# Two thirds of the converted weights are packed inside their own tile and stored from there

## The chip, the cores and the metric

The kernel runs on one core of one Trainium2 chip. The metric is the device time of one execution in microseconds (us). A core has TensorE (PE, with its weight loads shown apart as PEld), VectorE (DVE), ScalarE (ACT), GpSimd (POOL) and SyncE (SP). POOL and SP issue most of the DMAs here; each engine takes its instructions in order and stops at one whose semaphore has not come.

## The reference

```python
scores = np.where(masks, scale * q @ k.T, -1e9)      # 4 x 8 heads, 576 tokens, 64 wide; local and strided masks
x = softmax(scores) @ v                              # 2304 tokens x 512
h = x @ w_in;  g = s * np.maximum(h, 0) ** 2 + b     # 512 -> 2048
x = g @ w_out                                        # 2048 -> 512
x = ((x @ w_a) * (x @ w_b)) @ w_out2                 # 512 -> 1536, twice; 1536 -> 512
```

All of it is wanted in float32. The six weight arrays come as float64, so each weight is two 32-bit words, a low and a high one, that the kernel turns into one float32 word.

## The kernel before

TensorE multiplies each float32 operand as a high and a low part, three products a piece. The first MLP walks over five blocks of tokens (n = 0 to 4) and, in each, over 16 slices f of 128 hidden columns. For one slice `h_mm` (matmuls `h`) fills a PSUM bank; ACT takes it out with the relu into the one tile `r` (L802) and squares it into `gt` (L809); DVE makes the low part (L812, L813); and `o_mm` (matmuls `acc`) uses `gt` two slices later. In blocks 1 to 3 the bank of `h` is a single one, so the next slice's `h` waits for the relu before it, and the relu waits until L813 has freed `r`. Between the slices stand the steps of the attention of later tokens: `pss` (scores), softmax pieces on DVE and ACT (L437 to L451), `ppt` (transposes on PE), `po` (values), and copies of `po` into the next block's `x` (ACT L122, DVE L124).

Also between the slices of blocks 1 to 3, `convert_w2` turns the second MLP's weights into float32: 36 pieces of 128 rows, i = 0 to 35, in the order w_a, w_b, w_out2, w_a and so on, so that i % 3 tells the kind (2 is w_out2). One conversion is:

- a load of 512 KB from DRAM into a tile `raw` [128, 512, 2] on POOL's queue (L130 for w_a and w_b, L135 for w_out2). There are two such tiles, used in turn, and the load of piece i + 2 is issued right behind the store of piece i;
- ACT scales the high words in place (L142), DVE shifts the low words (L145), joins bits of both into the low words (L148), and packs both into one float32 word (L158);
- a store of 256 KB to DRAM (`w2d`) on POOL's queue (L865).

In the kernel before, L158 writes to a tile of its own, `w2s`, of which there is one. A piece's ACT and DVE instructions may not start before the last instructions of the slice that stands ahead of them (`behind`); otherwise the order on each engine comes from the framework's scheduler, when the program is built. From block 4 on the stored weights are read back and combined for the second MLP, whose matmuls are `pp` and `o`.

Of the kernel before, what the change touches and what calls it, by code (L numbers as in the profile page):

```python
# [12 lines left out]
U32 = mybir.dt.uint32  # L13
# [7 lines left out]
P = 128  # L21
# [6 lines left out]
def sparse_attention_two_mlps(  # L28
# [16 lines left out]
    NT, DM = out.shape  # L45
# [23 lines left out]
    hp = ctx.enter_context(tc.tile_pool(name="hp", bufs=1))  # L69
# [23 lines left out]
    w2s = [dram.tile([P, 2, 2, DM], F32, name=f"w2s{i}") for i in range(NF2)]  # L93
# [10 lines left out]
    @contextmanager  # L104
    def after(instructions):
        with ExitStack() as st:
            for i in instructions:
                st.enter_context(tc.issue_after(i))
            yield
# [16 lines left out]
    def stage(w, f, cols, pool, eng=nc.sync):  # L126
        r = pool.tile([P, DM, 2], U32, tag="w" if pool in (wpa, wpb, wpc) else "raw", name="raw")
        words = w.bitcast(U32)
        if cols:
            load = eng.dma_start(  # L130
                out=r.rearrange("p (k c) t -> p k (c t)", k=KD),
                in_=words[:, f * 2 * P:(f + 1) * 2 * P].rearrange("(k p) c -> p k c", p=P),
            )
        else:
            load = eng.dma_start(  # L135
                out=r.rearrange("p c t -> p (c t)"), in_=words[f * P:(f + 1) * P, :]
            )
        return r, load.ins

    def to_float32(r, out=None, quarters=False):  # L140
        low, high = r[:, :, 0], r[:, :, 1]
        nc.scalar.activation(  # L142
            out=high.bitcast(F32), in_=high.bitcast(F32), func=AF.Copy, scale=HIGH_SCALE
        )
        nc.vector.tensor_scalar(  # L145
            out=low, in0=low, scalar1=29, scalar2=None, op0=ALU.logical_shift_right
        )
        nc.vector.scalar_tensor_tensor(  # L148
            out=low, in0=high, scalar=3, in1=low, op0=ALU.logical_shift_left, op1=ALU.bitwise_or
        )  # L150
        out = high if out is None else out
        pieces_ = [(out, high, low)]
        if quarters:
            to = out.rearrange("p (r a i c) -> p a r i c", r=2, a=2, c=STR)
            low, high = (t.rearrange("p (r i a c) -> p a r i c", r=2, a=2, c=STR) for t in (low, high))
            pieces_ = [(to[:, a], high[:, a], low[:, a]) for a in range(2)]
        for to, high, low in pieces_:
            nc.vector.scalar_tensor_tensor(  # L158
                out=to, in0=high, scalar=0x80000000, in1=low, op0=ALU.bitwise_and, op1=ALU.bitwise_or
            )  # L160
        return out.bitcast(F32)
# [689 lines left out]
    def convert_w2():  # L851
        words = {}

        def load(i):
            if i < 3 * NF2:
                f, kind = divmod(i, 3)
                words[i] = stage((w_a, w_b, w_o2)[kind], f, kind < 2, raw, nc.gpsimd)[0]

        load(0)
        load(1)  # L860
        yield
        for i in range(3 * NF2):
            with after(list(behind)):
                w = to_float32(words.pop(i), hp.tile([P, DM], U32, tag="w", name="w2s"), i % 3 == 2)
            nc.gpsimd.dma_start(out=w2d[i], in_=w)  # L865
            load(i + 2)
            yield
# [219 lines left out]
    words = []  # L1087
# [56 lines left out]
    for what in ORDER.split():  # L1144
        name, of = what[:-1], int(what[-1])
# [8 lines left out]
    for f, piece in enumerate(pieces):  # L1154
        wi[f] = by_rows(piece.w)
    later = [Stream(convert_w2(), 3 * NF2 + 1, sum(T1[1:-1]) * NF1 - 3 * T1[-2])]
    for n in range(1, NB):
        plan(n)
# [300 lines left out]
    for pair in range(NP2):  # L1459
        quads = []  # L1460
        later_x.clear()
        for g in range(NG2):
            i = pair * NG2 + g
            kind = g % 2
            w = loaded[i]
# [121 lines left out]
```

## Time and profile before

| | us |
|---|---|
| median of 3 runs | 881.11 (880.87 to 881.37) |
| the profiled execution, its own time | 882.01 |
| its span, from the first instruction to the last | 880.2 |
| PE busy in the span | 870.9 |
| POOL busy in the span | 158.1 |

The profiled execution is 0.9 us above the median and its span leaves out 1.8 us around the program. In the views of the profile a group of rows gives busy time, the mean of one instruction and the idle time of its engine ahead of it, with the instruction or DMA that ended that idle time behind an arrow.

### The profile page before, as it was taken

How to read it: one execution, taken by the hardware profiler on the slowest of the kernel's cores; microseconds unless marked ns; L12 is line 12 of the kernel's file. 1: busy time of each engine (PE TensorE's matmuls, PEld its weight loads, DVE VectorE, ACT ScalarE, POOL GpSimd, SP SyncE). 2: the span in 40 equal slices, each digit the busy share in tenths (PEclk: the TensorE clock that was granted, in tenths of full speed). 3: DMA queues.
4: the chain of work that ended last, by engine and by line, in shares of the span. 5: the costliest groups of instructions: out<-in, count | busy, mean ns of one | idle time of the engine just before them, and what ended most of it. 6: DMA issues, size and time to landing. Idle time of an engine off the chain costs nothing.

```text
span 880.2 us, 17207 instructions
## 1 busy us (share of the span) xinstructions
PE 870.9 (99%) x6296; PEld 805.4 (92%) x6296; DVE 679.1 (77%) x1363; ACT 406.4 (46%) x872; POOL 158.1 (18%) x308
## 2 busy tenths in 40 slices
PE   8999999999999999999999999999999999999998
PEld 6778888999888899998888999999999999999998
DVE  6898996686767676847876798798877797887794
ACT  6777774443433343337665333463223463222261
POOL 6000001111112211114544000005400005200020
PEclk9999999999999999999999999999999999999999
DMA  9975543866685758458999668688668788766487
GB/s 213 289 236 151 173 85 105 186 163 165 170 201 151 178 173 188 140 169 281 351 317 338 197 207 261 216 256 263 203 198 278 251 252 260 211 200 206 150 259 217
DMA packets 173156, 187.21 MB, mean 213 GB/s; under 512 B 108880, under 2 KB 125648, under 8 KB 173072
## 3 DMA queue, kind: packets, MB, share of 16 engines
q1 hardware_dynamic: 147776, 119.90, 47.7%
q0 software_dynamic: 20096, 64.90, 22.4%
q10 hardware_dynamic: 5200, 1.31, 0.8%
q8 instruction: 50, 0.82, 0.4%
q14 instruction: 34, 0.28, 0.1%
HBM read 143.59 MB, written 42.47 MB: 211 GB/s over the span
## 4 chain that ended last, share of the span: by engine, by line
PE 96%; ACT 2%; DVE 1%; issue 0%; POOL 0%; ACTq 0%; POOLq 0%
PE pp L99 30%; PE h L99 23%; PE acc L99 22%; PE o L99 15%; PE po L99 2%; PE pss L99 1%; PE ppt L102 1%; PE fpo L99 1%; ACT fpt L620 1%; PE lull L99 0%; ACT raw L142 0%; PE fps L102 0%; PE pst L102 0%; ACT fqkT L620 0%; PE fpp L102 0%; PE fss L99 0%
## 5 line engine op out<-in xcount | busy, mean ns | idle before, releaser
L99 PE MATMUL pp<-x2w,wf 128*128 128x384 f32 x1296 | 230.9, 334 | 0.0
L99 PEld LDWEIGHTS pp<-x2w,wf 128*128 128x128 f32 x1296 | 225.2, 188 | 0.1
L99 PE MATMUL h<-x,w 128*128 128x512 f32 (+1 forms) x960 | 215.8, 373 | 0.0
L99 PE MATMUL acc<-gt,w 128*128 128x512 f32 (+2 forms) x960 | 210.7, 368 | 1.0 <-ACT w L122 1.0
L99 PEld LDWEIGHTS acc<-gt,w 128*128 128x128 f32 x960 | 175.5, 188 | 24.0 <-ACT w L122 1.4
L99 PEld LDWEIGHTS h<-x,w 128*128 128x128 f32 x960 | 172.5, 188 | 24.5 <-DVE w L124 0.5
L99 PE MATMUL o<-gf,o2w 128*128 128x384 f32 (+1 forms) x756 | 130.3, 333 | 0.7 <-issue 0.7
L99 PEld LDWEIGHTS o<-gf,o2w 128*128 128x128 f32 x756 | 129.6, 188 | 1.1 <-ACT gf L620 1.0
L802 ACT ACTIVATE r<-h 128x512 f32<-128x512 f32 (+1 forms) x80 | 44.3, 554 | 134.3 <-PE h L99 121.3
L620 ACT ACTIVATE gf<-quad 128x384 fp32r<-128x384 f32 x126 | 63.6, 522 | 84.4 <-DVE quad L625 61.6
L1343 POOL DMA_DIRECT2D out_dram<-ot x80 | 44.7, 567 | 249.4 <-DVE ot L1329 242.0
L625 DVE TENSOR_TENSOR gf<-quad,gf 128x384 fp32r<-128x384 f32 x126 | 67.6, 551 | 7.1 <-ACT gf L620 5.2
L812 DVE TENSOR_TENSOR r<-r 128x384 f32<-128x384 f32 (+1 forms) x48 | 28.9, 602 | 56.0 <-ACT gt L809 56.0
L625 DVE TENSOR_TENSOR quad<-pp,quad 128x384 f32<-128x384 f32 x108 | 59.8, 554 | 10.1 <-PE pp L99 8.4
L865 POOL DMA_DIRECT2D w2d<-w2s x36 | 19.7, 548 | 182.3 <-DVE w2s L158 155.7
L142 ACT ACTIVATE raw<-raw 128x512 f32<-128x512 f32 x66 | 42.6, 669 | 7.2 <-DMA raw<-in_moe_w_a_dram 3.3
L148 DVE SCALAR_TENSOR_TENSOR raw<-raw 128x512 uint32<-128x512 uint32 x66 | 44.5, 690 | 1.1
L620 ACT ACTIVATE wf<-wsrc 128x512 fp32r<-128x512 f32 x30 | 18.9, 629 | 54.1 <-PE pp L99 38.1
L99 PE MATMUL pp<-x2w,wh 128*128 128x384 f32 x216 | 43.2, 334 | 0.0
L620 ACT ACTIVATE quad<-pp 128x384 f32<-128x384 f32 x36 | 17.6, 490 | 54.3 <-PE pp L99 54.3
L625 DVE TENSOR_TENSOR quad<-quad 128x384 f32<-128x384 f32 x72 | 39.9, 554 | 1.3
L99 PEld LDWEIGHTS pp<-x2w,wh 128*128 128x128 f32 x216 | 38.0, 188 | 0.0
(191 smaller groups left out, 1011.9 us busy)
## 6 DMA issues: line engine op xcount, KB each, us to landing
o2w<-w2o SPq DMA_DIRECT2D x126, 256.0 KB
wf<-w2s SPq DMA_DIRECT2D x60, 512.0 KB
w2d<-w2s POOLq DMA_DIRECT2D x36, 256.0 KB, 2.6
w2r<-w2d POOLq DMA_DIRECT2D x36, 256.0 KB, 5.0
raw<-in_moe_w_in_dram SPq DMA_DIRECT2D x16, 512.0 KB
raw<-in_moe_w_out_dram SPq DMA_DIRECT2D x16, 512.0 KB
wsrc<-w2d SPq DMA_DIRECT2D x30, 256.0 KB
raw<-in_moe_w_a_dram POOLq DMA_DIRECT2D x12, 512.0 KB, 5.1
```

What stands on the lines that cost most here:

```text
L99: last_pe[:] = [nc.tensor.matmul(*args, **kwargs).ins]
L102: last_pe[:] = [nc.tensor.transpose(*args).ins]
L142: nc.scalar.activation(out=high.bitcast(F32), in_=high.bitcast(F32), func=AF.Copy, scale=HIGH_SCALE)
L148: nc.vector.scalar_tensor_tensor(out=low, in0=high, scalar=3, in1=low, op0=ALU.logical_shift_left, op1=ALU.bitwise_or)
L620: i = nc.scalar.activation(**kwargs).ins
L625: i = getattr(nc.vector, method)(**kwargs).ins
L802: relu = nc.scalar.activation(out=r, in_=ph, func=AF.Relu)
L812: nc.vector.tensor_tensor(out=r, in0=r, in1=r, op=ALU.mult)
L865: nc.gpsimd.dma_start(out=w2d[i], in_=w)
L1343: engines[k % len(engines)].dma_start(out=at.rearrange("(j t) c -> t j c", t=STR), in_=st[i * STR:(i + 1) * STR, j:j + m].rearrange("t j a ...
```

## The change

L158 of the w_a and w_b pieces (24 of 36) writes its 512 words to the first half of the piece's own tile `raw`, where words 2c and 2c + 1 held element c's low and high word, and the store reads from there. The w_out2 pieces (12) go through `w2s` as before.

```diff
@@ -861,7 +861,11 @@
         yield
         for i in range(3 * NF2):
             with after(list(behind)):
-                w = to_float32(words.pop(i), hp.tile([P, DM], U32, tag="w", name="w2s"), i % 3 == 2)
+                r = words.pop(i)
+                if i % 3 == 2:
+                    w = to_float32(r, hp.tile([P, DM], U32, tag="w", name="w2s"), True)
+                else:
+                    w = to_float32(r, r.rearrange("p c t -> p (c t)")[:, 0:DM])
             nc.gpsimd.dma_start(out=w2d[i], in_=w)
             load(i + 2)
             yield
```

On PE the order of instructions is the same in both programs. On POOL the order is the same too, and the semaphores that the rows wait for are others. Here are the stores and loads of pieces 26 to 30 in block 3, before; DMASW semaphores tell of the landing of POOL's DMAs, one after the other.

```order
L865 DMA w2d26_134<-w2s_4095 128x512 [waits DMASW6_49,DVE_49]
L130 DMA raw_4102<-in_moe2_w_b_dram 128x4x256 [waits DMASW3_49,Activation_49]
L180 COPY x_4321<-x_3226 128x8x64 [waits DMAHW1_49,DMAHW6_49,DMAHW0_49,DMAHW7_49,Activation_49,Pool_49]
L865 DMA w2d27_135<-w2s_4200 128x512 [waits DMASW0_49,DVE_49]
L135 DMA raw_4206<-in_moe2_w_out_dram 128x1024 [waits DMASW5_49,Activation_49]
L865 DMA w2d28_136<-w2s_4252 128x512 [waits DMASW2_49,DVE_49]
L130 DMA raw_4258<-in_moe2_w_a_dram 128x4x256 [waits DMASW7_49,Activation_49]
```

And of the changed program:

```order
L869 DMA w2d26_134<-w2s_4077 128x512 [waits DVE_49]
L130 DMA raw_4084<-in_moe2_w_b_dram 128x4x256 [waits DMASW3_49,Activation_49]
L180 COPY x_4301<-x_3216 128x8x64 [waits DMAHW1_49,DMAHW6_49,DMAHW0_49,DMAHW7_49,Activation_49,Pool_49]
L869 DMA w2d27_135<-raw_4028 128x512 [waits DMASW0_49,DMASW5_49,DVE_49,Activation_49]
L135 DMA raw_4187<-in_moe2_w_out_dram 128x1024 [waits DMASW0_49]
L869 DMA w2d28_136<-raw_4084 128x512 [waits DMASW7_49,DVE_49,Activation_49]
L130 DMA raw_4238<-in_moe2_w_a_dram 128x4x256 [waits DMASW2_49]
```

Load 29 (row L135) waited for ACT and for an earlier load; in the changed program it waits for DMASW0, which store 27, the row ahead of it, raises when it has landed. Load 30 waits for store 28 in the same way. Load 28, behind the w_out2 store 26, is as before. So it is for all 23 loads behind a store of w_a or w_b.

On ACT six of the 36 rows L142 have moved. Here is the stretch around piece 29 (w_out2) before, from the relu ahead of it to the second relu behind it:

```order
L802 ACTIVATE r_4273<-h_4260 128x384
L142 ACTIVATE raw_4206<-raw_4206 128x512
L809 ACTIVATE gt_4275<-r_4273 128x384
L122 ACTIVATE x_4321<-po_4292 128x128
L122 ACTIVATE x_4321<-po_4291 128x128
L555 ACTIVATE spT_4331<-ppt_4332 128x448
L122 ACTIVATE x_4321<-po_4292 128x64
L122 ACTIVATE x_4321<-po_4291 128x128
L802 ACTIVATE r_4360<-h_4347 128x384
```

And of the changed program:

```order
L802 ACTIVATE r_4253<-h_4240 128x384
L809 ACTIVATE gt_4255<-r_4253 128x384
L142 ACTIVATE raw_4187<-raw_4187 128x512
L122 ACTIVATE x_4301<-po_4272 128x128
L122 ACTIVATE x_4301<-po_4271 128x128
L122 ACTIVATE x_4301<-po_4272 128x64
L555 ACTIVATE spT_4311<-ppt_4312 128x448
L122 ACTIVATE x_4301<-po_4271 128x128
L802 ACTIVATE r_4340<-h_4327 128x384
```

L142 has gone behind L809, and L555 behind the third L122; pieces 3, 6, 9, 12 and 35 show the same exchange of L142 and L809. On DVE the order is the same, and the whole-width L158 no longer waits for a store. These are DVE's rows at piece 29, before:

```order
L145 TENSOR_SCALAR raw_4206<-raw_4206 128x512 [waits DMASW1_49]
L148 SCALAR_TENSOR_TENSOR raw_4206<-raw_4206 128x512 [waits DVE_49]
L158 SCALAR_TENSOR_TENSOR w2s_4338<-raw_4206 128x2x128 [waits DMASW2_49,DVE_49]
L158 SCALAR_TENSOR_TENSOR w2s_4338<-raw_4206 128x2x128
L124 TENSOR_TENSOR x_4321<-po_4292,x_4321 128x128 [waits DMAHW6_49,DMAHW1_49,DMAHW7_49,DMAHW0_49,Activation_49]
```

And of the changed program, where the store waited for is that of piece 26 and no longer that of piece 28:

```order
L145 TENSOR_SCALAR raw_4187<-raw_4187 128x512 [waits DMASW1_49,DMASW0_49]
L148 SCALAR_TENSOR_TENSOR raw_4187<-raw_4187 128x512 [waits DVE_49,Activation_49]
L158 SCALAR_TENSOR_TENSOR w2s_4318<-raw_4187 128x2x128 [waits DMASW6_49,DVE_49]
L158 SCALAR_TENSOR_TENSOR w2s_4318<-raw_4187 128x2x128
L124 TENSOR_TENSOR x_4301<-po_4272,x_4301 128x128 [waits DMAHW6_49,DMAHW1_49,DMAHW7_49,DMAHW0_49,Activation_49]
```

## Rows read from the trace of the kernel before

**Rows 1.** The page, busy us of each engine (share of the span) and instructions.

```profile
PE 870.9 (99%) x6296; PEld 805.4 (92%) x6296; DVE 679.1 (77%) x1363; ACT 406.4 (46%) x872; POOL 158.1 (18%) x308
```

**Rows 2.** Busy us by stretch: PE, PEld, DVE, ACT, POOL, then clock, DMA share, GB/s.

```profile
160.00:390.00 230.00, 229.99 (x2427) 207.82 (x2421) 163.96 (x339) 88.86 (x195) 44.25 (x73) 1.00 0.67 172
```

**Rows 3.** View of line L865, the 36 stores: ns each, first and last start, landing.

```profile
L865 POOL DMA_DIRECT2D w2d<-w2s x36: 547/547/560, 153.2 to 377.5; - x36
...
DMA to landing us min/median/max: 2.3/2.6/6.5
```

**Rows 4.** Views of lines L130 (from 120 us on) and L135: landing of the loads.

```profile
DMA to landing us min/median/max: 4.4/5.2/6.5
...
DMA to landing us min/median/max: 4.1/4.9/6.2
```

**Rows 5.** Waits of ACT from 120 to 400 us: total us, times, longest.

```profile
ACT r L802 <- PE h L99: 101.1, 44, 4.8
...
ACT raw L142 <- DMA raw<-in_moe_w_a_dram: 3.3, 4, 1.7
...
ACT raw L142 <- DMA raw<-in_moe_w_out_dram: 1.0, 1, 1.0
```

**Rows 6.** Timeline from 318 to 342 us: start, us, engine, line; pieces 25, 27, 29.

```profile
318.43 0.55 POOL L865 DMA_DIRECT2D w2d<-w2s  x1 [10.50 <-DVE w2s L158]
...
324.35 0.66 ACT L142 ACTIVATE raw<-raw 128x512 f32<-128x512 f32 x1
...
329.48 0.55 POOL L865 DMA_DIRECT2D w2d<-w2s  x1 [2.34 <-DVE w2s L158]
...
330.02 0.54 POOL L135 DMA_DIRECT2D raw<-in_moe_w_out_dram  x1
...
335.72 0.70 ACT L142 ACTIVATE raw<-raw 128x512 f32<-128x512 f32 x1 [0.99 <-DMA raw<-in_moe_w_out_dram]
...
337.34 0.55 ACT L555 ACTIVATE spT<-ppt 128x448 f32<-128x448 f32 x1 [0.18 <-PE ppt L102]
...
338.45 0.69 DVE L148 SCALAR_TENSOR_TENSOR raw<-raw 128x512 uint32<-128x512 uint32 x1
...
339.57 0.76 DVE L158 SCALAR_TENSOR_TENSOR w2s<-raw 128x256 uint32<-128x256 uint32 x2 [0.42 <-DMA w2d<-w2s]
340.25 1.12 DVE L124 TENSOR_TENSOR x<-po,x 128x128 fp32r<-128x128 f32 x4
...
340.94 0.49 ACT L802 ACTIVATE r<-h 128x384 f32<-128x384 f32 x1
...
341.47 2.05 PEld L99 LDWEIGHTS h<-x,w 128*128 128x128 f32 x12 [0.33 <-ACT r L802]
```

**Rows 7.** Views of single lines: landing of store 25, load 27, store 27, load 29.

```profile
DMA to landing us min/median/max: 2.3/2.3/2.3
...
DMA to landing us min/median/max: 4.5/4.5/4.5
...
DMA to landing us min/median/max: 3.5/3.5/3.5
...
DMA to landing us min/median/max: 5.7/5.7/5.7
```

**Rows 8.** Timeline from 346 to 366 us: store of piece 30, and piece 32.

```profile
348.68 0.55 POOL L865 DMA_DIRECT2D w2d<-w2s  x1 [6.74 <-DVE w2s L158]
...
354.04 0.69 ACT L142 ACTIVATE raw<-raw 128x512 f32<-128x512 f32 x1
...
362.32 0.69 DVE L451 TENSOR_TENSOR qk<-qk,sm 128x512 f32<-128x512 f32 x1
...
364.67 0.53 PEld L102 LDWEIGHTS ppt<-ident,qk 128*128 128x128 f32 x4
```

**Rows 9.** Views of single lines: landing of store 30, load 32.

```profile
DMA to landing us min/median/max: 2.5/2.5/2.5
...
DMA to landing us min/median/max: 4.8/4.8/4.8
```

## The prediction

> **What bounds the kernel now.** I read the page first: PE is busy in 870.9 of 880.2 us [rows 1]. The table by stretch then shows where the change lies: the 36 stores start between 153.2 and 377.5 us [rows 3], and from 160 to 390 us PE is busy in 229.99 of 230 us at full clock, while ACT has 88.86 and POOL 44.25 us of work [rows 2]. So the stage has nothing to give: work taken from DVE, ACT or POOL there can save at most the hundredths that PE stands idle, and the idle time outside is not touched. A delay is another matter, because PE has no slack of its own later in which to win a lost microsecond back. The question is only whether the change makes PE wait somewhere.
>
> Next come ACT's waits. The relu waits for PE 44 times, 101.1 us in total, so ACT is mostly early. But L142 waited for its load four times on w_a (longest 1.7 us) and once on w_out2 [rows 5]. These loads arrive just in time or late already; PE paid for none of that, since ACT was early. Last I read the timeline at the places with the least room [rows 6, 8].
>
> **What the change removes.** L158 no longer waits for the store before it. In the rows this wait shows at piece 29, 0.42 us on DVE [rows 6]. Behind it stand L124, L122 and a relu, and PE's weights for the next `h` stood 0.33 us for that relu [rows 6]. If piece 29's load came no later, this is the whole gain: 0.33 us. L158 itself does the same work, and L148, which already writes into `raw`, takes 0.69 us [rows 6]; I cost its new place at nothing. ACT's and POOL's instruction counts stay.
>
> **What it adds.** The load of piece i + 2 goes into the tile that store i reads. Before, the load was issued 0.54 us behind the store (329.48 and 330.02) [rows 6]. Now, for 23 loads, POOL stops until the store has landed: 2.3 to 6.5 us, median 2.6 [rows 3]. The load is issued about 2.0 us later, and 3 where the store took 3.5 [rows 7]. Behind the waiting load on POOL stands only the next store, some us away, so POOL itself loses nothing. The late load is waited for by ACT's L142 and DVE's L145 and L148; behind those stand the relu, L813 and the softmax pieces, on which PE's next `h` or `ppt` hangs. The loads concerned are those of w_out2 and w_a, which have the waits of [rows 5]. For most of them ACT's earliness covers it.
>
> **First place, `h` at 341.47.** Forwards from piece 25: its store starts at 318.43 and lands 2.3 us later, at 320.7 [rows 6, 7]. Load 27 goes out at 320.8 and takes 4.5 [rows 7], so L142 of piece 27 starts at 325.3 and not at 324.35 [rows 6]: 0.95 late. L809 and DVE's chain follow it, so store 27 starts at 330.4 and not at 329.48. It lands in 2.6 (median) to 3.5 (its own) [rows 3, 7], at 333.0 to 333.9. Load 29 goes out 0.1 later and takes 4.1 (the fastest w_out2 load) to 5.7 (its own) [rows 4, 7]: it lands between 337.2 and 339.7, against 335.7 before.
>
> Backwards from PE: with the new order on ACT, L142's start is followed by its 0.70, L148's 0.69, L158's two halves 0.76, then 0.69 from L124's start to the relu's (340.25 to 340.94), some 0.4 of L555 (0.55, partly beside L124) that now lies between, and 0.54 from the relu's start to the weights of `h` (340.94 to 341.47) [rows 6]: 3.8 us. PE was ready for these weights 0.33 before 341.47, at 341.14. So L142 may start up to 337.4 and costs nothing. The stall is 0 to 2.3 us. I take a store of 3.0 and a load of 4.9 (the median of its kind [rows 4]): landing at 338.4, a stall of **1.0**.
>
> **Second place, `ppt` at 364.67.** Store 30 starts at 348.68 and lands after 2.5 [rows 8, 9]. Load 32 goes out at 351.3 and takes 4.8 [rows 9]: L142 of piece 32 starts at 356.1 and not at 354.04. Behind it, in order, stand L809, the slice's DVE work, L145 to L158 and the softmax up to L451, which ended at 363.01, 1.66 us ahead of the weights of `ppt` [rows 8]. 2.05 late less 1.66 is **0.4**. With the fastest load (4.1) it is nothing, with the slowest (6.2) 1.8 [rows 4].
>
> **Elsewhere.** Twenty-one more loads come some 2 to 3 us later, and their landings vary from 4.1 to 6.5 us [rows 4], while the longest wait that cost PE nothing was 1.7 [rows 5]. Below, all are covered: nothing. Above, two more places pay like the first: 2.0. I take 0.8.
>
> Sum: 1.0 + 0.4 + 0.8 = 2.2 us. The profiled execution's own 882.01 becomes 884.2. It was 0.9 above the median of the runs, so for the median I say **883.3**, 0.25% over 881.11. About 0.2% (1.8 us) is what a measurement of this kernel can tell from no change, so this forecast lies near that line.
>
> **The rivals.**
>
> *The loads are quick once they are alone: no change.* Before, nearly every load started 0.54 us behind a store and shared the DMA engines with it; load 29 took 5.7 behind a store of 3.5 [rows 7]. Alone it may take 4.1, and then it lands at 337.2 to 338.1 with the stores above, and load 32 at 355.4: stalls of 0 to 0.7 and 0. With the 0.33 gained at best, the time is 880.8 to 881.8. It decides at a landing of 4.2 us for load 29 with a store of 2.6. Against it: load 27 took 4.5 and load 32 4.8 behind stores of 2.3 and 2.5, which were as good as done when the load's data moved [rows 7, 9].
>
> The Trainium skill, DMA: Bandwidth & Descriptors, section "Anatomy of one DMA — SWDGE (gpsimd) path", gives such a transfer a fixed 2.0 us and its bytes at 436 GB/s. By that a 512 KB load would take 3.2 us (an estimate), load 29 would land at 336.3 and load 32 at 354.6, both in time, and the kernel would stay at 881.1. For the 256 KB store it gives 2.6, which is the trace's median [rows 3]; for the load the trace has 4.1 at the least [rows 4], so the measurement decides against it. Of the chance of this rival I give the rule 0.05.
>
> *The conversion falls behind for good.* A tile `raw` is used every second piece. The pace is (377.5 - 153.2) / 35 = 6.4 us a piece [rows 3], 12.8 for two. From L142 to the store 5.1 us pass (324.35 to 329.48) [rows 6]; with a store of 2.6 and a load of 5.2 [rows 3, 4] that is 12.9, and 10.8 for the third use, which waits for no store. The mean, 12.2, leaves 0.6. With loads of 6.1 it would be 13.1, and 0.3 lost on each of 18 rounds is 5.4 us: 886.5 or more. For it speaks that SP's transfers stretched loads to 6.5 [rows 4]; against it, that the median is 5.2.
>
> *Faster.* The only way that the rows show is the 0.42 of DVE at piece 29, with 0.33 us to win and that only if load 29 lands by 337.4. That is within 0.2%.
>
> **How the numbers follow.** Chances: stalls at a few places, 1 to 5 us together, 0.63; all hidden, 0.27; behind for good, 0.08; something faster that no row shows, 0.02. Of the first, 0.50 lies over 1.8 us and 0.13 under. Slower is 0.50 + 0.08 = 0.58, same 0.13 + 0.27 = 0.40, faster 0.02. The range starts at no change, 881.1, where half of the hidden cases (0.13) lie below, and ends at the bounds of the three terms, 2.3 + 1.8 + 2.0 = 6.1 above, 887.2. The likeliest case alone runs from 882.1 to 886.5.
>
> **What would show it.** In the new profile POOL's loads of w_a and w_out2 start when a store has landed, 2.3 to 3.5 us behind its issue, and not 0.54. ACT's waits of L142 for w_a and w_out2 grow from 4.3 us to 15 or more. PE shows idle time ahead of `h` or `ppt` in the stretch to 390 us, most in block 3 around 341, with the relu or L451 as releaser; the stretch from 390 us on keeps its length. The prediction is wrong if loads alone land in about 4 us (no waits of PE), or if PE's waits spread over more than four places (rival two).

## The result: 887.1 us, 6.0 slower, from five places where PE waits

| | before | after |
|---|---|---|
| median, us | 881.11 (880.75 to 881.37, 5 runs) | 887.14 (885.60 to 890.28, 5 runs) |
| the profiled execution, own time | 882.01 | 887.14 |

The ratio is 1.0075 (95% interval 1.0052 to 1.0097, clear of 1): 6.0 us slower where 2.2 were forecast. The runs of the changed kernel also lie 4.7 us apart, those of before 0.6. In the profile of after the store is at L869, every other line named here as before.

The table by stretch (columns as in [rows 2]) has the loss in the stage of the conversions: PE was busy in 229.99 of the 230 us from 160 to 390 before, and now in 224.32.

```profile
160.00:390.00 230.00, 224.32 (x2305) 201.45 (x2298) 160.73 (x333) 87.25 (x191) 42.11 (x69) 1.00 0.63 168
```

PE's timeline (start, us, engine, line, operation; in brackets the idle time ahead of the row and its releaser) has these 5.67 us at five places:

```profile
312.33 1.16 PE L99 MATMUL h<-x,w 128*128 128x384 f32 x5 [0.37 <-DVE x L124]
...
332.75 2.37 PE L99 MATMUL h<-x,w 128*128 128x384 f32 x12 [0.96 <-ACT r L802]
...
339.00 0.63 PE L102 MATMUL ppt<-ident,sqk 128*128 128x128 f32 x4 [0.74 <-DVE sqk L451]
...
345.86 2.35 PE L99 MATMUL h<-x,w 128*128 128x384 f32 x12 [2.03 <-ACT r L802]
...
370.93 0.63 PE L102 MATMUL ppt<-ident,qk 128*128 128x128 f32 x4 [1.57 <-issue]
```

0.37 + 0.96 + 0.74 + 2.03 + 1.57 = 5.67. The fourth is the prediction's first place (`h` at 341.47 before), the fifth its second (`ppt` at 364.67). The first three are its "elsewhere".

ACT's waits from 120 to 400 us (columns as in [rows 5]) show what comes late. L142 waited 4.3 us for w_a and w_out2 before; it is 45.0 now, and the relu waits less for PE (58.2 against 101.1), which fits ACT having lost its lead.

```profile
ACT r L802 <- PE h L99: 58.2, 28, 3.8
ACT raw L142 <- DMA raw<-in_moe_w_a_dram: 27.6, 10, 4.6
ACT raw L142 <- DMA raw<-in_moe_w_out_dram: 17.4, 7, 3.8
ACT r L802 <- DVE gt L813: 17.3, 10, 4.1
```

On POOL's queue around piece 27 (answers to [rows 6]), load 27 (322.40) is issued 2.58 us behind store 25 (319.82) and not 0.54, since POOL waits until that store has landed. In the same way load 29 (337.61) follows store 27 (334.77), which landed in 2.6 us; the profile puts the end of that wait down to DVE's L813, but by the program the load waits for the store's semaphore alone.

```profile
319.82 0.55 POOL L869 DMA_DIRECT2D w2d<-raw  x1 [4.41 <-issue]
322.40 0.76 POOL L130 DMA_DIRECT2D raw<-in_moe_w_a_dram  x1 [2.03 <-DMA w2d<-raw]
325.40 0.55 POOL L869 DMA_DIRECT2D w2d<-w2s  x1 [2.25 <-DVE w2s L158]
325.94 0.76 POOL L130 DMA_DIRECT2D raw<-in_moe_w_b_dram  x1
...
334.77 0.55 POOL L869 DMA_DIRECT2D w2d<-raw  x1 [3.06 <-DVE mx L444]
337.61 0.54 POOL L135 DMA_DIRECT2D raw<-in_moe_w_out_dram  x1 [2.30 <-DVE gt L813]
```

What the prediction did not have is how long these transfers take. The DMA issues between 318 and 332 us (output, input, queue, count, KB, median us to landing) are single ones: load 27 takes 6.9 us (4.5 in [rows 7]), load 28 takes 8.9, store 26 takes 7.2.

```profile
raw<-in_moe_w_a_dram POOLq DMA_DIRECT2D x1, 512.0 KB, 6.9
raw<-in_moe_w_b_dram POOLq DMA_DIRECT2D x1, 512.0 KB, 8.9
...
w2d<-w2s POOLq DMA_DIRECT2D x1, 256.0 KB, 7.2
```

SP's timeline shows who else uses the DMA engines then: four stores of `o`, 256 KB each, at the end of block 2, and then loads of `q` and `k`. Before, load 27 was issued 2.7 us ahead of the first of these stores (318.97 and 321.67) and landed at 323.5; now it is issued 0.27 us ahead of it.

```profile
322.67 2.05 SPq L838 DMA_DIRECT2D o<-o1s  x4
326.76 3.38 SPq L285 DMA_DIRECT2D qk<-in_q_dram  x4
```

And this is how it reaches PE, on ACT and DVE:

```profile
324.25 0.51 ACT L802 ACTIVATE r<-h 128x384 f32<-128x384 f32 x1
329.37 0.67 ACT L142 ACTIVATE raw<-raw 128x512 f32<-128x512 f32 x1 [4.62 <-DMA raw<-in_moe_w_a_dram]
329.93 0.52 ACT L809 ACTIVATE gt<-r 128x384 fp32r<-128x384 f32 x1
...
332.21 0.49 ACT L802 ACTIVATE r<-h 128x384 f32<-128x384 f32 x1 [1.27 <-DVE gt L813]
...
330.48 0.56 DVE L812 TENSOR_TENSOR r<-r 128x384 f32<-128x384 f32 x1 [4.77 <-ACT gt L809]
331.15 0.97 DVE L813 TENSOR_TENSOR gt<-r,gt 128x384 fp32r<-128x384 f32 x1
```

The relu at 324.25 has its successor, the square L809, ready to run at 324.76. But L142 of piece 27 stands between them and waits 4.62 us for load 27. L812 and L813 wait for the square, `r` is free only behind L813, and so the next relu starts at 332.21 and PE's `h` at 332.75. Piece 27 is also stored late (334.77 against 329.48), load 29 lands late, and `h` pays again at 345.86.

### The profile page after: what moved, and what is told of

It is laid out like the page before. It is cut to its first block, busy times and chain, and to the rows that moved or that the text cites. A ratio compares the mean times of both kernels' runs of the same rounds, so it can differ in the third digit from the quotient of the medians.

```text
span 885.4 us, 17217 instructions
## 1 busy us (share of the span) xinstructions
PE 870.8 (98%) x6296; PEld 804.8 (91%) x6296; DVE 678.8 (77%) x1363; ACT 406.9 (46%) x872; POOL 157.7 (18%) x308
## 4 chain that ended last, share of the span: by engine, by line
PE 92%; DMA 2%; ACT 2%; DVE 1%; issue 1%; SPq 1%; ACTq 0%; DVEq 0%
PE pp L99 30%; PE h L99 21%; PE acc L99 20%; PE o L99 15%; PE po L99 2%; PE pss L99 1%; PE ppt L102 1%; PE fpo L99 1%; DMA raw<-in_moe_w_a_dram 1%; DMA fqk<-in_q_dram 1%; ACT raw L142 1%; DMA sv<-in_v_dram 0%; ACT fpt L620 0%; ACT r L802 0%; PE fss L99 0%
## 5 line engine op out<-in xcount | busy, mean ns | idle before, releaser
L802 ACT ACTIVATE r<-h 128x512 f32<-128x512 f32 (+1 forms) x80 | 44.3, 554 | 105.4 <-PE h L99 78.5
L812 DVE TENSOR_TENSOR r<-r 128x384 f32<-128x384 f32 (+1 forms) x48 | 28.8, 601 | 55.8 <-ACT gt L809 55.8
L142 ACT ACTIVATE raw<-raw 128x512 f32<-128x512 f32 x66 | 42.8, 673 | 50.2 <-DMA raw<-in_moe_w_a_dram 27.6
L148 DVE SCALAR_TENSOR_TENSOR raw<-raw 128x512 uint32<-128x512 uint32 x66 | 44.5, 690 | 2.8 <-ACT raw L142 1.9
L158 DVE SCALAR_TENSOR_TENSOR raw<-raw 128x512 uint32<-128x512 uint32 x54 | 36.0, 687 | 0.4
```

The costliest lines, as they stand in the source:

```text
L142: nc.scalar.activation(out=high.bitcast(F32), in_=high.bitcast(F32), func=AF.Copy, scale=HIGH_SCALE)
L148: nc.vector.scalar_tensor_tensor(out=low, in0=high, scalar=3, in1=low, op0=ALU.logical_shift_left, op1=ALU.bitwise_or)
L158: nc.vector.scalar_tensor_tensor(out=to, in0=high, scalar=0x80000000, in1=low, op0=ALU.bitwise_and, op1=ALU.bitwise_or)
L802: relu = nc.scalar.activation(out=r, in_=ph, func=AF.Relu)
L812: nc.vector.tensor_tensor(out=r, in0=r, in1=r, op=ALU.mult)
```

## The experiments

All medians stand beside the kernel before on the same chip (880.8 to 881.1 each time). The change itself is +6.0.

| kernel | median, us | ratio to before, 95% |
|---|---|---|
| e1_wait_only | 886.12 | 1.0054 (1.0041 to 1.0068) |
| e2_only_w_a_in_place | 881.43 | 1.0004 (0.9995 to 1.0013) |
| e3_only_w_b_in_place | 882.88 | 1.0023 (1.0010 to 1.0035) |
| e4_order_only | 880.78 | 1.0000 (0.9991 to 1.0008) |
| e5_keep_25_27 | 884.91 | 1.0045 (1.0032 to 1.0058) |
| e6_only_25_27 | 882.35 | 1.0018 (1.0009 to 1.0026) |
| e7_b_load_first | 885.72 | 1.0048 (1.0036 to 1.0060) |
| e8_all_wait | 890.18 | 1.0107 (1.0094 to 1.0120) |
| e9_keep_25_27_30 | 881.83 | 1.0007 (0.9998 to 1.0016) |
| e10_no_o_stores | 884.10 | 1.0033 (1.0023 to 1.0044) |
| e11_before_no_o_stores | 880.86 | 0.9996 (0.9987 to 1.0005) |
| e12_square_first | 881.00 | 0.9996 (0.9988 to 1.0005) |
| e13_square_first_27_28 | 884.39 | 1.0040 (1.0028 to 1.0052) |
| e14_square_first_27_28_30_32 | 881.88 | 1.0015 (1.0006 to 1.0024) |

### The late loads, or the packing in place, or the moved order?

**e1_wait_only.** The kernel before, with `w2s` for every piece. Behind a store of w_a or w_b POOL overwrites one word of `w2s`, which it can't do before the store has landed, and the load comes behind that.

```diff
-            load(i + 2)
+            landed = [nc.gpsimd.memset(w[:, 0:1], 0.0).ins] if i % 3 < 2 else []
+            with after(landed):
+                load(i + 2)
```

> The kernel before, with w2s as before, but behind each store of a w_a or w_b piece POOL clears one word of w2s, for which it must wait until the store has landed, and only then issues the load of piece i + 2. ACT's order is that of the changed kernel, nothing is packed in place; the cleared word is written over by the next piece. Late loads as the cause: 886 to 889, as the changed kernel. Packing or storing in place as the cause: 881, no change.

Measured: +5.1, with an interval that overlaps that of the change. The late loads, with every piece packed into `w2s`, bring the loss; that the place L158 writes to has a part in the last 0.9 us is not excluded.

**e4_order_only.** The kernel before, with L142 behind the square at pieces 3, 6, 9, 12, 29 and 35, as the change has it; `squared` holds the square of the slice ahead.

```diff
...
-            with after(list(behind)):
+            with after(behind + (squared if i in (3, 6, 9, 12, 29, 35) else [])):
```

> The kernel before, with nothing changed but ACT's order: L142 of pieces 3, 6, 9, 12, 29 and 35 stands behind L809 as in the changed kernel (L555 does not move). Late loads as the cause: 881, within 0.5. The moved order as the cause: 884 or more.

Measured: no difference. The rows that the change moved on ACT cost nothing.

### Which loads?

**e2_only_w_a_in_place** and **e3_only_w_b_in_place** pack one kind in place: in e2 the 12 w_out2 loads are late, in e3 the 11 w_a loads. The diff against the changed kernel is e2's; e3 has `i % 3 != 1`.

```diff
-                if i % 3 == 2:
-                    w = to_float32(r, hp.tile([P, DM], U32, tag="w", name="w2s"), True)
+                if i % 3 != 0:
+                    w = to_float32(r, hp.tile([P, DM], U32, tag="w", name="w2s"), i % 3 == 2)
                 else:
                     w = to_float32(r, r.rearrange("p c t -> p (c t)")[:, 0:DM])
```

> The changed kernel with w_a alone packed in place, so that the 12 loads of w_out2 alone wait for a store. If what costs is that late loads of w_a fall together with the w_out2 store and the w_b load behind it, little is left: 881 to 882.5. If each late load costs the same wherever it is, half: 884. If packing in place costs by itself, half too: 884.

> The changed kernel with w_b alone packed in place, so that the 11 loads of w_a alone wait for a store. If the pile of w_a load, w_out2 store and w_b load is what costs: 884 to 887, most of the loss, with the w_b loads over 6 us as in the changed kernel. If each late load costs the same: 884. Packing in place: 884.

Measured: +0.4 and +1.9 us, together 2.3, where both at once cost 6.0. e2 is as expected; e3 (882.88) is below each of its three expectations, although its w_b loads take 6.3 as a median: the pile by itself costs a third of the loss. The costs don't add up, which fits lateness that is handed on: piece 25 (w_b) makes load 27 (w_a) late, and piece 27, late itself, makes load 29 (w_out2) later still. With w_out2 loads late alone there is almost no loss (PE's waits from 140 to 400 us sum to 0.2): L142 of piece 29 started at 336.67, before the 337.4 that the prediction gave as the last moment.

### Which places?

**e5_keep_25_27** is the change with pieces 25 and 27 packed into `w2s` as before, **e6_only_25_27** the kernel before with these two alone in place, **e9_keep_25_27_30** is e5 with piece 30 in `w2s` too.

```diff
-                if i % 3 == 2:
-                    w = to_float32(r, hp.tile([P, DM], U32, tag="w", name="w2s"), True)
+                if i % 3 == 2 or i in (25, 27):
+                    w = to_float32(r, hp.tile([P, DM], U32, tag="w", name="w2s"), i % 3 == 2)
```

In e9 the list is (25, 27, 30); in e6 the condition is `i not in (25, 27)`.

> The change, but pieces 25 and 27 are packed into w2s as before, so loads 27 (w_a) and 29 (w_out2) do not wait for a store. Theory: the loss sits at the place around 331 to 342 us, where load 27, late, meets store 26 and load 28, and load 29 waits for a late store 27. Then PE's delays of 4.1 us there go (1.15 + 0.94 + 2.03) and those at 313 and 364.8 stay (0.8 + 1.7): 883.0 to 884.5. Rival, that the loss is spread evenly over the 23 late loads (0.26 each): 21 of 23 stay, 886.3 to 887.

> The kernel before, but pieces 25 and 27 alone are packed in place, so two loads are late, 27 and 29. Theory, if the place is a cause by itself: most of the 4.1 us at 331 to 342 comes, 883 to 885. If the lateness must be handed on from earlier pieces (21, 23) for the place to hurt: 881 to 882. Spread evenly: 2 of 23, 881.5.

> The change, but pieces 25, 27 and 30 are packed into w2s as before: loads 27, 29 and 32 do not wait, the other 20 do. Theory, that two places carry the loss: with both gone PE's delays in the stage are under 0.8 us and the time is 881.0 to 882.0. Rival, that each late load costs about the same: 20 of 23 stay, 884 or more (scaled from the 884.9 with 21).

Measured: e5 +3.9, where the places alone said +2 to +3.5 and an even spread +5.3 or more: between the two, nearer the first. In its profile (an execution of 883.09, the shortest of its five) the waits at 312 to 346 are gone, the 1.6 of `ppt` stands, and 0.5 has come up at the `h` two steps ahead of it (361 us). e6 gives +1.4, all of it at `h` (1.5 in its profile), and below the 883 to 885 that I expected: these two pieces alone are not all of that place; load 27 takes 4.9 us there, and piece 25 comes earlier than in the change (store at 318.30, not 319.82). e9 is the sharpest: with 20 of 23 loads still late, and L142 still waiting 31.5 us for w_a and w_out2, the time is back within 0.2% of before. These are PE's waits from 140 to 400 us in e9 (total us, times, longest), all of them:

```profile
PE ppt L102 <- issue: 0.2, 1, 0.2
```

So a late load costs nothing at most pieces. Taking three of 23 away takes nearly all of the loss away; two of the three by themselves cost 1.4 (e6).

### Who stretches the transfers?

**e7_b_load_first** exchanges the w_out2 store and the w_b load behind it on POOL's queue; **e8_all_wait** lets the w_b loads wait for their store too.

```diff
...
-            nc.gpsimd.dma_start(out=w2d[i], in_=w)
-            load(i + 2)
+            if i % 3 == 2:
+                load(i + 2)
+            with after(list(loaded) if i % 3 == 2 and i + 2 < 3 * NF2 else []):
+                nc.gpsimd.dma_start(out=w2d[i], in_=w)
+            if i % 3 < 2:
+                load(i + 2)
```

Here `loaded` holds the load issued last.

> The change, with the order of the store of a w_out2 piece and the w_b load behind it exchanged on POOL's queue (11 times); nothing else moves. Theory, that the late w_a load, the w_out2 store and the w_b load stretch each other and that the stretched w_b load is what PE pays for: the w_b load gets ahead of the store, its median falls from 6.5 to 5.5 us or less, and the time falls to 882.5 to 885.5. Rival, that the lateness of the w_a and w_out2 loads alone is paid for: 886 to 888, as the change.

```diff
-            load(i + 2)
+            landed = [nc.gpsimd.memset(w[:, 0:1], 0.0).ins] if i % 3 == 2 else []
+            with after(landed):
+                load(i + 2)
```

> The change, and the 11 w_b loads wait for their store too (a one-word memset of w2s on POOL behind the store, which cannot run before the store has read it). Theory of the pile-up: the w_b load is alone, its median falls from 6.5 to 4.0 to 4.7 us, while it starts 3 to 4.5 later, so that it lands about when it did: 885.5 to 888.5. Rival, that every waiting load costs the same (6.0 / 23 = 0.26 us): 11 more make 889 to 891.

Measured: e7 +4.7, between the two expectations, and its runs (883.2 to 886.4) reach from one to the other: it decides nothing, although the median of the w_b loads fell to 5.6. e8 is +9.2 (890.18, in the range of the rival that every waiting load costs the same, which e9 excludes), and my theory that load 27, store 26 and load 28 stretch each other is refuted. The w_b load alone does take 4.6 us (median 4.5, as expected), but load 27 and store 26 take what they took in the change, with no w_b load beside them. The DMA issues of e8 between 318 and 340 us:

```profile
raw<-in_moe_w_a_dram POOLq DMA_DIRECT2D x1, 512.0 KB, 6.9
raw<-in_moe_w_b_dram POOLq DMA_DIRECT2D x1, 512.0 KB, 4.6
w2d<-w2s POOLq DMA_DIRECT2D x1, 256.0 KB, 7.1
```

Something else is in their way. **e10_no_o_stores** moves SP's four stores of `o` from the end of block 2 to that of block 0, and **e11_before_no_o_stores** does the same to the kernel before.

```diff
-            nc.sync.dma_start(out=o1[e * P:(e + 1) * P, C1[n]:C1[n] + T], in_=o)
+            for m in {0: (0, 2), 2: ()}.get(n, (n,)): nc.sync.dma_start(out=o1[e * P:(e + 1) * P, C1[m]:C1[m] + min(T, T1[m])], in_=o[:, 0:min(T, T1[m])])
```

> The change, and the four 256 KB stores of `o` that SP issues at 322.7 us, at the end of block 2 (L838), are taken away there: those rows of `o` are written at the end of block 0, with block 0's values, so the tokens of block 2 are computed from other numbers. Theory, that the late load 27 is stretched to 6.9 us because it now meets these stores: load 27 lands in 4.5 to 5.0, load 29 starts 2 us earlier, PE's 4.1 us at 331 to 342 shrink by half or more, 882.5 to 884.5. Rival, that load 27, store 26 and load 28 stretch each other without SP: load 27 stays over 6, 886 to 888.

> The kernel before with the same stores of `o` moved to the end of block 0 (tokens of block 2 computed from other numbers): the control. PE does not wait at this place before, so both theories say 880.5 to 881.5.

Measured: 884.10 (+3.0, half of the loss gone) and 880.86 (no difference). In e10's profile PE waits 0.81 us at 341.66 where the change has four waits from 312 to 346, but another 0.87 at 361.97; the first of those four (0.37 at 312.33) stands before SP's stores, so the profiles do not split the 3.0 cleanly. In e10 the same load 27 and store 26 take 3.9 and 2.8 us, load 28 still 6.8. Its DMA issues between 318 and 332 us:

```profile
raw<-in_moe_w_a_dram POOLq DMA_DIRECT2D x1, 512.0 KB, 3.9
raw<-in_moe_w_b_dram POOLq DMA_DIRECT2D x1, 512.0 KB, 6.8
w2d<-w2s POOLq DMA_DIRECT2D x1, 256.0 KB, 2.8
```

Load 27 and store 26 are stretched by SP's stores, then. The other traces add how close the call is. Where load 27 was issued 0.26 or 0.27 us ahead of the first of these stores (the change, e8, e13, e14), it took 6.8 to 6.9 us; where it was 0.41 to 0.63 us ahead (e1, e3, e6, e7), it took 4.7 to 4.9. The two rows in e6:

```profile
320.88 0.76 POOL L130 DMA_DIRECT2D raw<-in_moe_w_a_dram  x1 [2.03 <-DMA w2d<-raw]
321.29 2.35 SPq L838 DMA_DIRECT2D o<-o1s  x4
```

So the long load 27 is one part of the loss and not the whole: e1 costs 5.1 with a load 27 of 4.9 in its profile. The Trainium skill, DMA: Bandwidth & Descriptors, section "Queues, rings and completion order", says that each DMA engine takes turns between the queues that have work for it; the runs agree, in that POOL's transfers take 3.0 and 4.4 us longer with SP's beside them; the turns themselves, and why so little lead decides over some 2 us, no run here shows.

### By what way does the lateness reach PE?

**e12_square_first** is the change with every L142 behind the square L809 of the slice ahead; **e13** and **e14** do that at two and at four pieces only. Lines count one more in these kernels up to the relu (L142 is L143, L802 is L803) and two more at the square (L811).

```diff
...
-                nc.scalar.activation(out=hi, in_=r, func=AF.Square)
+                square = nc.scalar.activation(out=hi, in_=r, func=AF.Square)
...
-            with after(list(behind)):
+            with after(behind + squared):
```

In e13 the last line is `with after(behind + (squared if i in (27, 28) else [])):`, in e14 with (27, 28, 30, 32).

> The change, with every L142 put behind L809 of the slice ahead of it, so that a late load no longer holds up the square and L812 and L813 behind it. PE and POOL keep their order; ACT moves at some 35 places and DVE at some 20 (L148 and L158 one or two rows later). If the lateness reaches PE by L809 and L813: 882 to 884.5. If it reaches PE by the DVE work and the relu that stand behind L142, L145 and L148 themselves: 885.5 to 888.5.

> The change, with L142 of pieces 27 and 28 alone put behind L809 of the slice ahead (ACT changes at two places, DVE at one). Theory, that a late load reaches PE through the square L809 that stands behind the waiting L142, with L812, L813 and the next relu behind it: PE's delays at 331 and 336 us (1.15 and 0.94 us in the profile of the change) go and that at 341 (2.03) shrinks, because piece 27 is converted earlier; the one at 364.8 stays: 883 to 885. Rival, that the exchange of all 35 in e12_square_first worked in another way (DVE's other order): 886 to 888.

> The same for pieces 30 and 32 too. Theory: the delay of ppt at 364.8 us goes as well, 881.2 to 883.0. Rival: 885 or more.

Measured: e12 881.00, no difference from before, and better than the 882 to 884.5 of my theory. All 23 loads still wait for their stores. ACT's timeline around piece 27 in e12:

```profile
323.71 0.49 ACT L803 ACTIVATE r<-h 128x384 f32<-128x384 f32 x1 [0.50 <-PE h L100]
324.23 0.53 ACT L811 ACTIVATE gt<-r 128x384 fp32r<-128x384 f32 x1
324.69 0.67 ACT L143 ACTIVATE raw<-raw 128x512 f32<-128x512 f32 x1
...
337.22 0.68 ACT L143 ACTIVATE raw<-raw 128x512 f32<-128x512 f32 x1 [2.80 <-DMA raw<-in_moe_w_out_dram]
```

The square runs right behind its relu, and L143 of piece 27 needs no wait: store 25 went out at 317.70 and load 27 at 320.27, 1.23 us before SP's first store of `o` (321.50), and took 4.3 us. That fits earlier squares not having been held up. Piece 29 starts at 337.22, again just before 337.4, after 2.80 us of waiting that cost PE nothing.

e12 moved some 35 rows on ACT and load 27 no longer met SP's stores, so e13 and e14 ask at single pieces. e13 is +3.6 (884.39, as the theory had it). It keeps 6.8 us for load 27 and a wait of 3.82 us at L143 of piece 27, and still the waits at 332 and 339 are gone; the one at `h` (341.47 before) is 3.1, not smaller as I expected, because load 29 came late all the same. PE's waits in e13, from 140 to 400 us, all of them:

```profile
PE h L100 <- ACT r L803: 3.1, 1, 3.1
PE ppt L103 <- issue: 0.5, 1, 0.5
```

e14 has +1.1 us left of 6.0, within its 881.2 to 883.0. But its twelve runs fall into two groups, eight from 880.5 to 882.5 and four from 883.7 to 885.0, and its profile is of the longest (885.01): there `ppt` waits no more, and `h` has 3.1 as in e13. The runs near 881 cannot hold that wait in full; none of them was profiled. The way through the square is shown, then, for pieces 27 and 28 (e13); for 30 and 32 e14's median and its missing `ppt` wait speak for it. Piece 29, where L142 stands behind its square already, pays by the DVE work and relu behind it.

e14's profile shows one more price of a wait. Behind the 3.11 us at `h` the clock granted to TensorE stood at 0.50, the lower of its two levels (1.2 GHz), from 344.5 to 347.5 us, and the 12 matmuls took 3.91 us. In e13, behind 3.09 us, it stayed at 1.00 and they took 2.36. These are the row of e14, the stretch from 345 to 346 us in it (columns as in [rows 2]), and the row of e13:

```profile
343.99 3.91 PE L100 MATMUL h<-x,w 128*128 128x384 f32 x12 [3.11 <-ACT r L803]
345.00:346.00 1.00, 1.00 (x5) 1.00 (x4) 0.64 (x2) 0.00 (x0) 0.00 (x0) 0.50 0.88 229
344.40 2.36 PE L100 MATMUL h<-x,w 128*128 128x384 f32 x12 [3.09 <-ACT r L803]
```

## Why the prediction was wrong

The direction and the mechanism were right; all three terms of the sum were too small, 2.2 us for 6.0.

- **PE has no slack and nothing to win: right.** No kernel's ratio lies below 0.9996.
- **The load waits for the store, some 2 us later: right** (2.58 for 0.54 at load 27), and e1 shows that this is the cause.
- **The last moment for L142 of piece 29, 337.4: right within 0.7 us.** At 336.67 (e2) and 337.22 (e12) `h` did not wait for the relu; at 338.16 (e6) it waited 1.5 (0.8 by that reckoning).
- **The step that failed at the first place: "Load 27 goes out at 320.8 and takes 4.5".** First place, forecast 1.0: 2.03. The 4.5 is a row of before, where load 27 was issued 2.7 us ahead of SP's stores of `o`. In the change it was issued 0.27 us ahead of them and took 6.9. It landed at 329.3 and not at 325.3, store 27 was issued at 334.77 and not at 330.4, load 29 landed at 342.1 and not between 337.2 and 339.7. The "store of 3.0 and a load of 4.9" behind it held (2.6 and 4.5). In e6, where load 27 took 4.9, the sum comes out almost as forecast: L142 of piece 29 at 338.16 (338.4 forecast), a wait of 1.45. e10 shows what SP's stores cost: 3.0 of the 6.0.
- **The step that failed at the second place: "Store 30 starts at 348.68".** Second place, forecast 0.4: 1.57. This too is a row of before, in which load 30 was not late; but load 30 is one of the 23 and waits for store 28. In e5, where PE had not yet waited, store 30 starts at 351.27, L142 of piece 32 at 357.98 and not at 356.1, and PE pays 0.55 and 1.56. e9, where load 32 does not wait for store 30, has 0.2 left.
- **Elsewhere, 0.8: measured 2.07** (0.37 + 0.96 + 0.74), past its bound of 2.0. I looked for the price of load 27 at piece 29 alone. But L142 of piece 27 itself stands on ACT between a relu and its square, so a wait of 4.6 there holds L809, L812, L813 and the next relu. The prediction named this order ("L809 and DVE's chain follow it") and priced it only for the next store. e13 shows it for pieces 27 and 28.
- **The range.** The two places came out within their bounds (2.3 and 1.8), near the upper end, and "elsewhere" past its own (6.1 by the bounds, 5.67 in the profile). The terms were summed at their middles as if each were late by itself; they share late loads, so they can be large together. That 887.14 lies 0.06 below the range's end of 887.2 is luck; the runs lie on both sides of it.
- **The rival "loads are quick once alone": half right.** The w_out2 loads fell from a median of 4.9 to 4.0 us and alone cost nothing (e2). By the estimate of 3.2 us from the Trainium skill, DMA: Bandwidth & Descriptors, section "Anatomy of one DMA — SWDGE (gpsimd) path", they would be quicker yet; the shortest one that waited took 3.6 (e5), 3.8 in the change, so the measurement stays above it. The w_a loads are not always alone: load 27 runs into the next store and into SP.
- **The rival "falls behind for good" gave the nearer number (886.5) for a reason that does not hold.** In e9 20 of 23 loads are late and 881.83 is left. The conversion catches up between the places: in the change L142 of pieces 25, 26, 33 and 34 waited for no load.
- **The sign named for being wrong came true:** PE's waits lie at five places, not at four or fewer.

What stays open: why 11 more waits cost 3.2 us more (e8), which was not followed piece by piece; how much of the 0.75 us left in e9 is real; and why the change's runs lie as far apart as 885.6 and 890.3, of which one was profiled. That landing times differ from run to run would fit, and so would a fall of the clock as in e14's profile: the granted clock is 0.998 in four of the change's five runs and 1.000 in the profiled one, and in e3 the two runs at 886.5 are the only ones with 0.998. Neither was shown for the change.

## What to carry to other kernels

A duration read from a trace belongs to its moment: before moving a transfer by 2 us, look at what the other queues send in the place where it will land, and price it with that beside it. Where many transfers become late, start each sum from a late one too. On an engine that works in order, a wait costs what stands behind it; so put an instruction that may wait for a DMA behind the work on which the busy engine depends: here the late loads then cost nothing (e12, 881.0 against 887.1). And terms of one chain can be late together: sum their upper ends as one case too, not their middles alone.

## What the runs showed of the hardware

The DMA issues of the changed kernel from 153 to 385 us, medians of each kind:

```profile
w2d<-raw POOLq DMA_DIRECT2D x24, 256.0 KB, 2.6
raw<-in_moe_w_out_dram POOLq DMA_DIRECT2D x12, 512.0 KB, 4.0
raw<-in_moe_w_a_dram POOLq DMA_DIRECT2D x11, 512.0 KB, 5.3
raw<-in_moe_w_b_dram POOLq DMA_DIRECT2D x11, 512.0 KB, 6.5
w2d<-w2s POOLq DMA_DIRECT2D x12, 256.0 KB, 4.7
```

The same 512 KB took 4.0 us where the load followed a landed store (w_out2), 6.5 where it was issued 0.54 us behind a store and beside a late load (w_b), and 8.9 with SP's stores as well; 256 KB of store took 2.3 to 7.2. Making loads wait made those of w_out2 quicker (4.9 to 4.0), those of w_a not in this trace (5.0 to 5.3) but in e1 and e12 (4.5 and 4.6), and what is issued behind a late w_a load slower (w_b loads from 5.6 to 6.5, w_out2 stores from 3.0 to 4.7). I had expected a load that waits for its store to run alone; it can meet others instead.
